# A fused attention and maxout kernel: its hand-ordered queue planned anew, with bias products as units of their own and twelve staging buffers

## The chip, the cores and the metric

The kernel runs on one core of a Trainium2 chip. The metric is device microseconds of one execution. Its engines are TensorE (PE; its weight loads are shown as PEld), VectorE (DVE), ScalarE (ACT), GpSimd (POOL) and SyncE (SP), whose queue here issues nearly all DMAs. Each engine works through its own instructions in the order in which the program emits them, and waits on semaphores where an instruction needs what another engine has not yet done.

## What is computed

The reference, cut to what matters, is windowed attention with a linear distance bias, followed by a feed-forward layer with the maximum of three products:

```
# q, k, v: [4, 8, 768, 64]; n_global = 8, n_local = 96
scores = q @ k.T / sqrt(64)
rel = i - j;  is_local = 0 <= rel < 96;  is_global = j < 8
dist = 96 where (is_global and not is_local), else |rel|
scores = scores - slope[head] * dist          # slope[h] = 2 ** -(h + 1)
a = softmax(scores where (is_global or is_local) else -1e9)
x = (a @ v) as [3072 tokens, 512]
h = max(x @ w1, x @ w2, x @ w3)               # w*: [512, 768]
out = h @ w_out                               # [3072, 512], fp32
```

## The kernel before

The 3072 tokens are 24 tiles of 128 (six for each of the four batches). The feed-forward layer takes them in seven chunks, `SIZES = [4, 2, 2, 4, 4, 4, 4]` tiles. All the work is cut into units, and the string `SCHEDULE` (line 24) lists every unit in the order of emission; the last loop of the kernel function reads a unit's letter, its numbers and, behind `@`, the number of the buffer it takes, and calls the function of that letter. So the string fixes the order on every engine and all the buffers. It was made by a planner outside the kernel, from costs of the units. The units (first numbers: G is a group of two tiles, T a tile, g one half of the heads, c a chunk, f one of six blocks of 128 hidden columns, j which of w1, w2, w3; a last number without a point of its own is the engine: 0 ScalarE, 1 VectorE, 2 GpSimd):

- `l`: load of q (0), k (1) or v (2) of a group; group 12 ("quad") is tiles 0 to 3 of q and k in four loads of 0.5 MB. `c`: its cast to bf16; on GpSimd a cast is two instructions. `v`: cast of v into the tile's buffer.
- `x` (TensorE) and `y` (copy): transposes of q and k; from group 5 on `X`, a DMA transpose on SP, does both.
- `K`, `B`: masks and biases of a head, at the start. `S`: scores of a tile and half of the heads. With its last number 1, two matmuls with the identity first put the bias into the two PSUM banks; without it, `m` multiplies the mask in after the exponential. `e`: exponential (ScalarE).
- `G`, `V`: put the first keys and values of the batch into a tile's buffers, after the tile's own S or A has read them and before the next tile's.
- `A`: probabilities times values. `n`: reciprocal and scaling (VectorE). `t` and `u`, or the DMA transpose `Z` on SP: the transpose that makes x ready for the chunk's F.
- `w`, `q`: loads of the weights (w0.j is 0.5 MB, w1.j is 1 MB, q 0.5 MB); `W`, `Q`: their casts.
- `F`: four matmuls, into one bank. `f` with j = 0 casts the bank to SBUF, with j = 1 takes the maximum with it, with j = 2 the maximum again, into the chunk's hidden buffer.
- `O`: six matmuls, an output tile. `o`: its copy into a staging buffer. `s`: its store, on SP; with a last 2, in two halves. `E`: the output tiles of the last chunk; the last of them is cut into columns of 256, 128 and 128, and the last copy and store are ScalarE's own.
- `D`: matmuls of zeros at the start. `R`: the distances.

PSUM has eight banks. F, O, x and t take one, A and S take two; a bank can be taken again once its last reader is done. Staging buffers of the outputs are slices of the buffers `wst0` and `wst1`, into which the weights were loaded (three each).

## Time and profile before

| | |
|---|---|
| median of 3 runs | 176.38 us (176.31 to 176.66) |
| the profiled execution's own time | 176.6 us |
| its span, first to last instruction | 174.7 us |
| granted TensorE clock | 1.000 |
| DMA | 37.35 MB, mean 214 GB/s |

In a profile, a group of instructions is given by line, engine, operation, tile and shape, with the number of them, the busy time and the mean duration of one in ns, and then the time that the engine idled before them and what ended it. In a timeline the first number is the start in us, the second how long the merged instructions took. A matmul's busy time includes its drain, so that two matmuls in a row overlap in it.

### The profile page before, as it was taken

To read this page: it belongs to the slowest core of one execution; us is meant where nothing else is said; L and a number is where in the kernel's file an instruction comes from. 1 tells how busy PE (TensorE), PEld (TensorE's weight loads), DVE (VectorE), ACT (ScalarE), POOL (GpSimd) and SP (SyncE) were. 2 spreads that over 40 slices of the span, in tenths; PEclk is the share of its full clock that TensorE was granted. 3 is DMA by queue.
4 is the path that set the end of the run, shared out by engine and by line. 5 is a ranking of instruction groups with operands and counts; after the bars stand their busy time and mean duration, and the time that the engine had idled before them with its cause. 6 is when DMAs were issued, how large, how long until landed. Compare 5 with 4: busy or idle time off the path is not lost.

```text
span 174.7 us, 3862 instructions
## 1 busy us (share of the span) xinstructions
PE 166.9 (96%) x1489; PEld 93.5 (54%) x1510; DVE 127.7 (73%) x259; ACT 102.4 (59%) x153; POOL 48.9 (28%) x94
## 2 busy tenths in 40 slices
...
GB/s 148 352 292 312 363 351 379 294 319 345 270 230 267 193 145 194 290 319 198 232 146 196 119 253 200 290 159 260 272 184 68 32 90 64 0 180 240 60 10 234
DMA packets 66658, 37.35 MB, mean 214 GB/s; under 512 B 24144, under 2 KB 61904, under 8 KB 66640
## 3 DMA queue, kind: packets, MB, share of 16 engines
...
q8 instruction: 12, 0.20, 0.5%
q10 hardware_dynamic: 144, 0.07, 0.1%
q14 instruction: 6, 0.05, 0.1%
...
## 4 chain that ended last, share of the span: by engine, by line
PE 83%; DVE 5%; DMA 4%; ACT 3%; issue 2%; SPq 1%; ACTq 0%
PE psum L405 50%; PE psum L429 18%; PE psum L321 5%; DMA rawqq<-in_q_dram 4%; PE psum L363 4%; PE psum L366 3%; PE psum L258 2%; DVE qkT L266 1%; ACT P L328 1%; PE psum L390 1%; DVE h L421 1%; DVE P L337 1%; PE psum L313 1%; SPq L213 1%; ACT qb L185 1%
## 5 line engine op out<-in xcount | busy, mean ns | idle before, releaser
L405 PE MATMUL psum<-xT,w 128*128 128x512 bf16 (+1 forms) x491 | 99.3, 348 | 1.1
L405 PEld LDWEIGHTS <-w 128*128 128x128 bf16 x504 | 47.5, 98 | 43.1 <-issue 2.7
L328 ACT ACTIVATE P<-psum 128x1024 bf16<-128x1024 f32 (+1 forms) x48 | 43.3, 953 | 13.5 <-PE psum L321 13.2
L421 DVE TENSOR_TENSOR h<-h,psum 128x512 bf16<-128x512 bf16 (+1 forms) x42 | 24.6, 604 | 16.1 <-PE psum L405 12.6
L429 PE MATMUL psum<-wo,ht 128*128 128x512 bf16 (+2 forms) x148 | 32.9, 362 | 0.6 <-issue 0.3
L337 DVE TENSOR_TENSOR P<-P,wmask 128x1024 bf16<-128x1024 bf16 x35 | 23.8, 695 | 6.2 <-ACT P L328 6.1
L424 DVE TENSOR_TENSOR ht<-h,psum 128x512 bf16<-128x512 bf16 (+1 forms) x42 | 26.1, 643 | 3.0 <-PE psum L405 2.4
L419 ACT CAST h<-psum 128x512 bf16<-128x512 f32 (+1 forms) x32 | 15.6, 517 | 20.1 <-PE psum L405 17.9
L429 PEld LDWEIGHTS <-ht 128*128 128x128 bf16 x156 | 14.0, 98 | 14.1
L238 POOL CAST va<-rawv 64x512 bf16<-64x512 f32 x26 | 16.5, 636 | 13.6 <-DMA rawv<-in_v_dram 12.8
L375 DVE TENSOR_TENSOR xb<-psum,rz 128x512 bf16<-128x512 f32 x24 | 16.6, 691 | 0.8
L299 POOL COPY va<-vaf 4x260 int32<-4x260 int32 x15 | 5.9, 395 | 37.5 <-PE psum L366 37.2
L321 PE MATMUL psum<-qkT 64*128 64x128 bf16 x352 | 14.9, 217 | 1.2 <-DVE qkT L266 0.9
L321 PEld LDWEIGHTS <-qkT 64*128 64x128 bf16 x352 | 10.3, 94 | 9.6 <-issue 6.8
L363 PEld LDWEIGHTS <-P 128*128 128x128 bf16 x192 | 12.3, 97 | 2.4
L363 PE MATMUL psum<-va,P 128*128 128x65 bf16 x160 | 12.5, 193 | 0.1
L444 ACT COPY ost<-psum 128x512 f32<-128x512 f32 x11 | 6.4, 589 | 8.9 <-PE psum L429 8.2
L366 PEld LDWEIGHTS <-P 128*128 128x128 bf16 x160 | 10.4, 97 | 1.5 <-issue 0.3
L434 ACT COPY ost<-psum 128x512 f32<-128x512 f32 (+2 forms) x5 | 2.3, 480 | 15.1 <-PE psum L429 15.0
L366 PE MATMUL psum<-va,P 128*128 128x65 bf16 x128 | 9.9, 193 | 0.0
L301 ACT COPY va<-vaf 4x520 bf16<-4x520 bf16 x10 | 6.2, 620 | 3.8 <-PE psum L366 3.7
L374 DVE RECIPROCAL rz<-psum 128x8 f32<-128x8 f32 x24 | 4.8, 202 | 4.7 <-PE psum L366 3.7
...
## 6 DMA issues: line engine op xcount, KB each, us to landing
rawv<-in_v_dram SPq DMA_DIRECT2D x12, 512.0 KB, 6.3
rawq<-in_q_dram SPq DMA_DIRECT2D x10, 512.0 KB, 7.3
rawk<-in_k_dram SPq DMA_DIRECT2D x10, 512.0 KB, 7.0
...
wst<-in_moe_w_dram SPq DMA_DIRECT2D x3, 512.0 KB, 8.1
wost<-in_moe_w_out_dram SPq DMA_DIRECT2D x3, 512.0 KB, 7.3
out_dram<-ost SPq DMA_DIRECT2D x9, 128.0 KB, 1.8
```

Of the source, the lines that this page charges most:

```text
L238: copies[how](heads(va(T))[64 * e:64 * e + 64, :, 0:D], src)
L321: nc.tensor.matmul(sp[:, hh, j2, ds], qT(T - ds, 1)[hsl, jp], qT(T, 0)[hsl, jp], start=not how, stop=True, skip_group_check=True)
L328: nc.scalar.activation(P[:, :, 0:n], sps[T, g].rearrange("p a b d n -> p (a b) d n")[:, :, 0:n], AF.Exp, bias=0.0, scale=scale)
L337: mul(P, P, wmask[:, g, :, 0:2])
L363: nc.tensor.matmul(o, P[:, i, 0], heads(va(T))[:, h], start=True, stop=(t == 0), skip_group_check=True)
L366: nc.tensor.matmul(o, P[:, i, 1], heads(va(T - 1))[:, h], start=False, stop=True, skip_group_check=True)
L375: nc.vector.tensor_tensor(out=x.rearrange("p (g h) d -> p g h d", g=2), in0=o4[:, :, :, 0:64], in1=rz[:, :, :, None].to_broadcast([128, 2, ...
L405: nc.tensor.matmul(ps, w123[f // 2][:, j, dm, (f % 2) * 128:(f % 2) * 128 + 128], xT[c][:, dm], start=(dm == 0), stop=(dm == 3))
L419: copies[how](h01, ps)
L421: nc.vector.tensor_max(h01s[c, f], h01s[c, f], ps)
L424: nc.vector.tensor_max(dst, h01s[c, f].rearrange("p (t e i) -> p t e i", e=2, i=64), ps.rearrange("p (t e i) -> p t e i", e=2, i=64))
L429: nc.tensor.matmul(po, ht[c][:, f, tt * 128:(tt + 1) * 128], wo[:, f, cols], start=(f == 0), stop=(f == NF - 1))
```

## The change

1. A new unit `b` holds the two bias matmuls. `S` with a last number 1 takes the buffer of its `b`; seven groups have one, as before, but tile 0 has one (it had two) and tile 1 has two (it had one).
2. Outputs are staged in a ring `os` of 12 buffers, which lie in one tile with `wst0` and `wst1` (over the place of `wst1`). E takes twelve in turn too.
3. Groups 0 and 1 keep q and k in an order with the half of the heads outside the tile, so that `y` writes one piece.
4. The whole string is another. The planner that made it now holds each buffer until the instruction that reads it last has ended.

Both strings hold the same units but for the seven `b`; tile 8 goes by `Z` and no longer by `t`, and tile 7 the other way (before: tiles 0 to 6, 8 and 11 by `t`; after: 0 to 7 and 11). Counts by engine:

| unit | before: ScalarE, VectorE, GpSimd | after |
|---|---|---|
| `c` cast of q, k | 9, 7, 8 | 5, 6, 13 |
| `v` cast of v | 8, 6, 34 | 10, 6, 32 |
| `y` copy of transposes | 8, 6, - | 5, 9, - |
| `G` | 4, 6, 10 | 7, 10, 3 |
| `V` | 10, 7, 15 | 12, 4, 16 |
| `u` | 3, 6, - | 5, 4, - |
| `f` with j = 0 | 32, 10, - | 24, 18, - |
| `o` | 11, 9, - | 10, 10, - |
| `W` | 2, 4, 3 | 1, 4, 4 |
| `Q` | 1, -, 2 | -, -, 3 |
| `B` | 2, 6, - | 3, 5, - |

The diff, cut (of the string: the start with the first loads and the first F, chunk 3's F, and the end):

```diff
-    l0.12.1@0 l1.12.1@1 R K4 K3 K6 B4.1 B0.1 K5 K0 K2 B1.0 K7 B6.0 B2.1 l1.12.0@2 B3.1 c0.12.1.1@0 B7.1
-    l0.12.0@3 l2.0.2@0 l2.1.2@1 l0.2.2@4 c1.12.1.1@1 l1.2.2@5 w0.1@0 B5.1 D10.512@0 w0.0@1 x12.0.1@0
...
-    v2.1.1 v2.0.1 A0@0 n0@0 v3.0.2 l2.2.2@2 w1.1@1 A1@4 V1.1.2 e2.0@5 v3.1.2 n1@1 S3.0.1@6 c0.2.2.0@2 V1.0.1
-    S3.1.1@0 w1.2@2 t1@2 c1.2.2.1 u1.1@0 e3.0@6 A2@4 n2@2 x2.0.2@3 V2.1.2 V2.0.2 x2.1.2@2 G3.2 y2.1.2.1@2
-    e3.1@7 l1.3.2@6 A3@0 t2@4 l0.3.2@0 y2.0.2.0 W0.1.2 n3@3 t0@3 u2.0 S4.0.0@6 u0.1 e4.0@1 S4.1.0@4 t3@2
-    u3.1 W0.0.1 G4.2 S5.0.0@0 W0.2.2 e5.0@3 S5.1.0@6 m5.0.1 V3.1.0 e5.1@0 m5.1.1 m4.0.1 W2.0.1 v5.0.2 e4.1@2
-    W1.0.1 F0.0.1@2 F0.1.1@3 F0.0.0@0 f0.0.0.0@0 F0.1.0@1 F0.0.2@4 F0.1.2@0 f0.1.0.0@1 F0.4.0@1 v5.1.2
...
-    V22.0.2 n22@0 O4.3@1 V22.1.0 A23@2 n23@3 Z22 O5.3@0 o5.3.0@2 O5.2@4 O5.1@0 O5.0@2 o5.0.0@0 Z23 F6.2.0@3
...
-    f6.0.1.1 f6.0.2.1 f6.3.2.1 s4.0.2 s4.3.2 s5.2.2 F6.5.0@0 f6.5.0.1@0 F6.5.1@3 f6.5.1.1 F6.5.2@1 f6.5.2.1 E@0
+    l1.12.1@0 l0.12.1@1 R B6.1 K6 K7 B1.1 B4.0 K4 B3.1 K1 K5 c1.12.1.1@0 B7.1 B5.0 K3 K2 B2.1 l0.12.0@2
+    l1.12.0@3 D10.512@0 x12.1.1@0 l2.0.2@0 v1.1.2 v1.0.2 v0.1.2 c0.12.1.1@1 D3.256@1 x12.0.1@1 b1.1@2
+    l2.1.2@1 y1.1.1.1@0 b2.1@4 v0.0.2 c0.12.0.1 x12.0.0@6 y0.1.1.1@1 y0.0.1.0 S1.1.1 y1.0.1.0 B0.0 S0.1.0@0
...
+    l0.2.2@5 w1.0@0 w0.1@0 G0.1 m0.1.1 G1.1 b0.0@2 S0.0.1 e1.0@2 v3.1.2 v3.0.2 b2.0@6 e0.0@3 v2.1.1 S2.0.1
+    e2.0@4 v2.0.1 l2.2.2@2 K0 S2.1.1 e2.1@5 w0.0@1 b3.1@0 w0.2@2 w1.1@1 A0@2 G2.1 n0@0 S3.1.1 e3.1@6 A1@6
+    n1@1 b3.0@2 S3.0.1 w1.2@2 c1.2.2.2@2 V1.0.1 c0.2.2.2 e3.0@7 x2.1.2@4 V1.1.1 A2@0 t0@5 y2.1.2.1@2 t1@6
+    n2@2 V2.0.0 x2.0.2@4 y2.0.2.1 u0.0@0 G3.0 u1.0 V2.1.2 A3@2 V3.1.2 l1.3.2@6 n3@3 t2@5 S4.0.0@0 S4.1.0@6
+    l0.3.2@0 V3.0.2 G4.2 l1.4.2@1 e4.0@0 u2.1 t3@4 W2.0.2 u3.0 W1.0.1 m4.0.1 e4.1@3 S5.0.0@2 l2.3.2@0
+    l0.4.2@2 S5.1.0@0 W0.1.1 e5.1@1 m4.1.1 v4.0.2 e5.0@2 v4.1.2 F0.3.0@4 F0.5.0@5 f0.5.0.0@0 F0.4.0@6
...
+    m13.0.1 l1.8.2@2 v15.0.2 F3.4.0@3 F3.1.2@5 l0.8.2@4 v12.0.2 v15.1.2 F3.1.0@4 F3.1.1@2 A12@0 f3.1.0.1@4
+    f3.1.1.1 n12@1 m13.1.1 F3.0.0@4 c0.7.2.1@0 l0.9.2@3 F3.2.0@2 f3.4.0.1@2 f3.0.0.1@0 F3.0.1@0 v16.1.1
+    c0.8.2.2@2 c1.7.2.0 A13@6 F3.4.1@1 F3.2.2@3 f3.1.2.1@1 F3.5.0@4 F3.5.1@5 f3.0.1.1 f3.4.1.1 X14@3
+    F3.2.1@0 f3.2.0.0@3 F3.4.2@1 c0.9.2.2@1 f3.5.0.1@1 l1.9.2@5 f3.5.1.1 n13@0 F3.3.0@2 X15 f3.4.2.1
+    f3.2.1.1 f3.2.2.1 S14.0.0@4 e14.0@5 v17.0.2 S14.1.0@6 F3.0.2@0 F3.3.2@1 f3.3.0.1@4 m14.0.1 f3.0.2.1
+    F3.5.2@2 l2.9.2@0 v16.0.1 c1.9.2.0 e14.1@6 Z13@1 c1.8.2.2 F3.3.1@0 G14.0 S15.0.0@4 e15.0@0 S15.1.0@6
...
+    f5.0.2.1 m23.1.1 f5.5.1.1 A23@5 n22@1 f5.5.2.1 n23@2 f5.2.2.1 O4.3@0 F5.3.2@1 s0.2 s1.0 Z22 O4.2@5
+    f5.3.2.1 O5.3@1 O5.0@2 o5.0.1@0 Z23 o4.2.1@11 o5.3.1@10 O5.1@3 o4.3.1@8 s4.0 F6.0.2@2 F6.2.1@1 F6.0.0@0
...
+    s5.1 s0.0 F6.2.2@7 s5.0 f6.2.2.1 F6.4.2@1 s4.2.2 s5.3.2 s4.3.2 f6.4.2.1 F6.1.2@0 F6.5.0@3 f6.0.2.1
+    f6.1.1.1 F6.5.1@1 f6.1.2.1 F6.5.2@2 f6.5.0.0@2 f6.5.1.1 f6.5.2.1 E@7 O5.2@2 o5.2.0@1 s5.2.2
...
-RINGS = {'r': 7, ... 'wst0': 3, 'wst1': 3, 'ht': 2, 'h01': 5, 'rz': 4}
-LAST_BANKS = (7, 6, 4, 5, 2, 0, 3, 1)
-LAST_STAGES = ((2, 1, 0), (2, 0, 1))
+RINGS = {'r': 7, ... 'wst0': 3, 'wst1': 3, 'ht': 2, 'h01': 5, 'rz': 4, 'os': 12}
+LAST_BANKS = (5, 4, 7, 6, 3, 0, 1, 2)
+LAST_STAGES = (6, 9, 2, 5, 3, 7, 4, 0, 11, 10, 8, 1)
...
+    staging = persist.tile([128, 2048 * RINGS["wst1"] + 1024 * RINGS["wst0"]], FP32, name="staging")
+    staged = {"wst1": (0, 2048), "os": (0, 512), "wst0": (2048 * RINGS["wst1"], 1024)}
...
+            shape = [128, 2, 2, 2, NP // 2, 128] if G < 2 and QUAD_USED else [128, 2, 2, NP, 128]
...
-    def u_S(slot, T, g, how):
-        t = T % NT
+    def u_b(slot, T, g):
+        n = 2 if T % NT else 1
         sp = ring("sp", slot, [128, 2, 2, 2, 128], FP32, "sp")
         sps[T, g] = sp
-        n = 2 if t else 1
-        biased[T, g] = how
-        if how:
-            for hh in range(2):
-                nc.tensor.matmul(sp[:, hh, :, 0:n], identb,
-                                 bias[:, g, hh, :, 0:2] if t else bias[:, g, hh, :, 2:3],
-                                 start=True, stop=False, skip_group_check=True)
+        for hh in range(2):
+            nc.tensor.matmul(sp[:, hh, :, 0:n], identb, bias[:, g, hh, :, 0:2] if n == 2 else bias[:, g, hh, :, 2:3],
+                             start=True, stop=False, skip_group_check=True)
+
+    def u_S(slot, T, g, how):
+        n = 2 if T % NT else 1
+        biased[T, g] = how
+        if not how:
+            sps[T, g] = ring("sp", slot, [128, 2, 2, 2, 128], FP32, "sp")
+        sp = sps[T, g]
...
-        osts[c, tt] = ring(("wst0", "wst1")[chunks[c][tt] % 2], slot, [128, DM], FP32, "ost")
+        osts[c, tt] = ring("os", slot, [128, DM], FP32, "ost")
```

More of the change, by code (lines that the diff above doesn't have):

```diff
@@ L157, in ring @@
         assert 0 <= slot < RINGS[name]
+        if name in staged:
+            first, width = staged[name]
+            first += slot * width
+            flat = staging[:, first:first + math.prod(shape[1:])]
+            return flat if len(shape) == 2 else flat.rearrange("p (i f) -> p i f", i=shape[1])
         return pools[name].tile(shape, dtype, name=label, tag=f"{name}{slot}")
```

143 lines of the change are left out of this document (73 added, 70 removed).

## The prediction

> **What bounds the kernel now.** I read the page's first part, then its chain, then the timeline of TensorE.
>
> ```profile
> span 174.7 us, 3862 instructions
> PE 166.9 (96%) x1489; PEld 93.5 (54%) x1510; DVE 127.7 (73%) x259; ACT 102.4 (59%) x153; POOL 48.9 (28%) x94
> ...
> PE 83%; DVE 5%; DMA 4%; ACT 3%; issue 2%; SPq 1%; ACTq 0%
> ...
> L405 PEld LDWEIGHTS <-w 128*128 128x128 bf16 x504 | 47.5, 98 | 43.1 <-issue 2.7
> ...
> rawk<-in_k_dram SPq DMA_DIRECT2D x10, 512.0 KB, 7.0
> ```
>
> TensorE is busy for 96% of the span and is 83% of the chain that ended last. "Busy" hides short waits, because a matmul counts until it is drained, so I compare the work with the clock instead.
>
> ```profile
> 1.19 4.45 PE L506 MATMUL psum<-zeros 128*128 128x512 bf16 x10 [1.19 <-DVE cap L524]
> 5.60 0.77 PE L252 MATMUL psum<-identb,qbq 128*128 128x128 bf16 x8
> ...
> 21.52 7.94 PE L405 MATMUL psum<-xT,w 128*128 128x512 bf16 x35
> 29.31 0.19 PE L363 MATMUL psum<-va,P 128*128 128x65 bf16 x1
> ...
> 29.79 2.75 PE L405 MATMUL psum<-xT,w 128*128 128x512 bf16 x11
> ...
> 37.73 0.61 PE L258 MATMUL psum<-identb,qb 128*128 128x128 bf16 x8
> 38.18 1.47 PE L405 MATMUL psum<-xT,w 128*128 128x256 bf16 x12
> ...
> 72.66 2.53 PE L405 MATMUL psum<-xT,w 128*128 128x512 bf16 x10
> ...
> 118.58 9.16 PEld L405 LDWEIGHTS <-w 128*128 128x128 bf16 x43 [0.20 <-issue]
> ```
>
> ```profile
> 52.86 0.22 PE psum L390 x4
> ...
> 98.71 0.55 PE psum L321 x16
> ...
> 169.63 1.93 PE psum L429 x20
> ```
>
> In an unbroken run 43 weight loads take 9.16 us: (9.16 - 0.098) / 42 = 0.216 us for a matmul of 512 columns. The 504 matmuls of F (144 of them half as wide) and the 24 output tiles of six are 576 such widths: 124.3 us. From the first F, at 21.52 us, to the last matmul, at 171.55, there are besides 15 tiles of S at 0.55 us and three of half that (9.1), 17 A at 29.79 - 29.31 = 0.48 and three halves (8.9), four x at 0.45 (1.8) and five t at 0.22 (1.1). Together 145.2 us of 150.0: only **4.8 us** are lost in the body. The rest of the span is 21.5 us of start and 3.1 us of tail.
>
> **The change, part by part.** *Work.* Both queues hold the same units: 126 F, 24 output tiles, 48 S, 24 A, 10 x, 9 t. So TensorE's 145.2 us stand, and only start, losses and tail can move. Bias products: two of the seven groups covered tile 0 (half width), now one does, so two matmuls grow by 256 columns: 2 x 0.108 = 0.2 us, issued while TensorE waits for casts: nothing.
>
> *Start.* ScalarE and VectorE set it.
>
> ```profile
> 10.00:15.00 5.00, 4.58 (x67) 2.49 (x67) 4.43 (x9) 4.31 (x8) 3.59 (x7) 1.00 1.20 290
> 15.00:20.00 5.00, 4.99 (x97) 3.62 (x94) 4.83 (x12) 4.69 (x6) 3.33 (x8) 1.00 1.11 341
> ```
>
> ```profile
> 15.40 1.05 ACT L185 CAST qb<-rawq 128x1024 bf16<-128x1024 f32 x1
> 16.34 1.95 ACT L328 ACTIVATE P<-psum 128x1024 bf16<-128x1024 f32 x2
> ...
> 20.90 0.42 DVE L393 COPY xT<-psum 128x512 bf16<-128x512 bf16 x1 [0.30 <-PE psum L390]
> ...
> 11.20 1.88 DVE L266 COPY qkT<-psum 128x512 bf16<-128x512 bf16 x3
> ...
> 22.38 1.69 POOL L185 CAST w<-wst 128x512 bf16<-128x512 f32 x2 [1.67 <-DMA wst<-in_moe_w_dram]
> ...
> 32.09 1.05 ACT L185 CAST w<-wst 128x1024 bf16<-128x1024 f32 x1 [1.45 <-DMA wst<-in_moe_w_dram]
> ```
>
> (Windows: busy us of TensorE, weight loads, VectorE, ScalarE, GpSimd.) VectorE is busy for 9.3 and ScalarE for 9.0 of these 10 us. The first F waits for the last u of chunk 0, which hangs on e of tile 3 (ends 18.29). The new queue gives the cast of q of group 2 (1.05 us, ScalarE) to GpSimd and puts one more bias row (about 0.4) and one G less (0.2) on ScalarE: e3 ends near 17.45. Then ScalarE has V2, u0, G3, u1 and e4.0 (0.6 + 0.55 + 0.2 + 0.55 + 0.95, estimates from row means less 0.05 of overlap) before u3 (0.59): F could start at about 20.9. But the 1 MB load w1.0 now stands ahead of the three w0 loads and feeds the first F. The old queue's landings, from the two casts that wait for them: 5.5 MB (counted from the first load) at 22.38 us, 9 MB at 32.09, so 2.8 us for a MB; w1.0 is complete at 5 MB, 21.0 us, and its cast takes 0.7: 21.7. Between 20.6 and 21.7 I take 21.1: **-0.4 us** (ends -0.9, +0.2). The later weights stay at 9 MB, so this lead cannot grow by them.
>
> *F of chunks 0 to 2 (to 72.66 us).* Work there by the same prices is 49.2 us of 51.1: 1.9 lost. I followed the new queue by hand, bank by bank, with the row means: TensorE waits about 1.4 us by whole durations, less where instructions overlap (three copies of 0.682 take 1.88 us: 0.60 apart). With 0.1 at each of six entries to S I take 1.4: **-0.5** (ends -1.3, +0.5). Holding a buffer until its reader has ended is a rule for the planner: it removes no instruction, and pays only where an S or F now waits for a bank.
>
> *F of chunk 3.* Five of six first casts of a bank (f with j = 0) go to VectorE, before it was one; ScalarE idles there.
>
> ```profile
> L337 DVE TENSOR_TENSOR P<-P,wmask 128x1024 bf16<-128x1024 bf16 x35 | 23.8, 695 | 6.2 <-ACT P L328 6.1
> L424 DVE TENSOR_TENSOR ht<-h,psum 128x512 bf16<-128x512 bf16 x30 | 21.0, 724 | 2.6 <-PE psum L405 2.1
> L421 DVE TENSOR_TENSOR h<-h,psum 128x512 bf16<-128x512 bf16 x30 | 19.9, 681 | 15.0 <-PE psum L405 12.6 <-ACT h L419 2.0
> ...
> L419 DVE CAST h<-psum 128x512 bf16<-128x512 f32 x9 | 6.2, 684 | 1.4 <-PE psum L405 1.3
> ```
>
> From the first F3 to the one before the last, VectorE has 5 casts (3.4), 5 maxima (3.4), 4 results (2.9), 2 n (1.8), 3 m (2.1), a cast (0.7), a v (0.5) and 1.3 left over from chunk 2: 16.1 us. TensorE has 17 F, two A and an S: 15.9. By whole durations VectorE is the bound, and the walk gives 1.9 us of waiting, most of it where F3.0.2 wants the bank that the maximum f3.2.1 reads; at 0.07 less for each of 24 it has 14.4 us and hides. Nearest row: three copies at 0.60, so the second: **+0.2** (ends 0, +1.9). In the same stretch ScalarE's cast c1.9 waits for a load that SP issues behind the transpose X14; queued behind the cast is e14.1, and S15.1 waits for its banks. By the load's median landing that is covered, by 2 us more it is not: it stays inside the upper end.
>
> *Chunks 4 and 5.*
>
> ```profile
> xT<-xb SPq DMA_TRANSPOSE x15, 3.6
> ```
>
> Covers are as thin as before: after A19 both queues have six F (5.2 us) for n19 and the transpose of its result (3.6 us to landing); X20 now has five stores ahead of it on SP's queue. **0** (ends -0.6, +1.2).
>
> *Last chunk and tail.*
>
> ```profile
> 150.29 16.05 PE L405 MATMUL psum<-xT,w 128*128 128x512 bf16 x71
> ...
> 155.62 3.33 PEld L405 LDWEIGHTS <-w 128*128 128x128 bf16 x16 [0.27 <-issue]
> ...
> 163.59 2.25 PEld L405 LDWEIGHTS <-w 128*128 128x128 bf16 x11 [0.25 <-issue]
> ...
> 171.63 0.27 ACT L434 COPY ost<-psum 128x128 f32<-128x128 f32 x1 [0.34 <-PE psum L429]
> 171.93 0.37 ACTq L435 DMA_DIRECT2D out_dram<-ost  x1
> ...
> 141.39 0.57 SPq L450 DMA_DIRECT2D out_dram<-ost  x1
> ```
>
> ```profile
> L444 ACT COPY ost<-psum 128x512 f32<-128x512 f32 x11 | 6.4, 589 | 8.9 <-PE psum L429 8.2 <-ACT P L328 0.7
> ...
> out_dram<-ost SPq DMA_DIRECT2D x9, 128.0 KB, 1.8
> ```
>
> From 150.29 to 171.55 us stand 18 F and four output tiles, 96 widths: 20.7 of 21.3 us, so 0.5 is lost, at gaps like the two quoted. In the new queue, walked in the same way, one wait of 0.15 is left: **-0.4**. But output tile O5.2 now comes behind E, whose last tile was cut into pieces of 256, 128 and 128 columns to end early. Before: last matmul, 0.08, copy 0.27, issue, 1.8 to landing: 2.2 us. After: 0.08, a whole copy of 0.59, a store of two halves, the second issued 0.55 later, and 1.8: 3.1. **+0.9** (ends +0.6, +1.2). The twelve staging buffers relieve stores that nothing waited for: 0.
>
> Sum: -0.4 - 0.5 + 0.2 + 0 - 0.4 + 0.9 = -0.2 us. The profiled execution took 176.6 us (span 174.7 and 1.9 around it), 0.2 above the median of 176.38; on the median the forecast is **176.2**.
>
> **A rule to weigh.** GpSimd gets 14 more casts (c, W, Q).
>
> ```profile
> L185 POOL CAST w<-wst 128x512 bf16<-128x512 f32 x6 | 4.5, 769 | 2.7 <-DMA wst<-in_moe_w_dram 2.7
> ...
> L185 POOL CAST wo<-wost 128x512 bf16<-128x512 f32 x4 | 2.3, 610 | 2.3 <-DMA wost<-in_moe_w_out_dram 2.3
> ```
>
> One shape takes 0.61 or 0.77 us: something holds it up by 0.16. The Trainium skill (SBUF — State Buffer, Who interferes with whom) says that GpSimd shares a port pair with VectorE as an exclusive lock, so that one of two overlapping instructions stands still; these rows fit that. If many of the casts were held for a whole VectorE instruction, the sum by that rule would be that of the third rival.
>
> **The rivals.** *VectorE takes over in chunk 3* (slower): the 1.9 us instead of 0.2: 176.2 + 1.7 = 177.9. It decides once its 24 instructions stand 15.9 / 24 = 0.66 us apart. For: five casts moved; against: 0.60 in the row above. 0.18.
> *Losses nearly vanish* (faster): 4.8 us down to 15 entries to S at 0.11 (1.7), start -0.9, tail +0.9: -3.1, with half a microsecond that stays: 173.8. For: buffers held to the reader's end are what the waits in the trace are about; against: DMA covers stay thin. 0.23.
> *GpSimd late:* 16 instructions from the landing of w1.2 to the cast of the last w_out at 0.16 each come 2.6 us late; the first output tile, by my walk, has about 1.5 of cover: 176.2 + 1.1 = 177.3. 0.08.
> *The early load of w1.0 buys nothing* (the change does not do what it says): F starts at 21.7 and the reordering wins nothing by chunk 2's end: 176.2 + 0.6 = 176.8. 0.09.
>
> **How the numbers follow.** Forecast 0.42, spread about 175.3 to 177.1. About 0.2%, 0.35 us, is what a measurement can tell. Faster: 0.17 of the forecast and 0.23: 0.40. Same: 0.14 and 0.03: 0.17. Slower: 0.11, 0.18, 0.08, 0.06: 0.43. The range takes half of the fast rival and most of the slow one: 173.6 to 178.3; the likeliest case alone 175.3 to 177.1.
>
> **What would show it.** First L405 matmul at 20.6 to 21.7 us; first F3 before 72.3; VectorE under 4.9 of 5 us through F3; the last matmul 3.9 to 4.2 us before the end of the span (now 3.1); no PE wait for POOL. A single wait of over 1 us on a transpose (X20, Z19, Z15) or on a load that ScalarE awaits (c1.9 before e14.1) would make it wrong.

## The result, and the profile after

The changed kernel is slower: its median is 177.1 us (20 runs, 176.52 to 179.39) beside 176.56 us for the kernel before (20 runs, 176.21 to 177.12), a ratio of 1.0043 with a 95% interval of 1.0026 to 1.0060. The profiled execution took 177.0 us with a span of 175.1, at a granted clock of 1.000. The ratios count fast executions only, which leaves out those over 1.5% above the fastest of their kernel (the one at 179.39 us here, and the profiled one of e2_g_scalar below, whose clock, 0.990 on the mean, fell in one slice behind 53 us and of which, but for the issue of one store, only rows ahead of that are used).

The page of the changed kernel, first its engines, then the shares of the chain that ended last:

```profile
span 175.1 us, 3856 instructions
PE 165.8 (95%) x1489; PEld 93.4 (53%) x1510; DVE 136.0 (78%) x268; ACT 93.7 (54%) x145; POOL 56.4 (32%) x100
...
PE 74%; DVE 15%; issue 3%; DMA 3%; ACT 2%; ACTq 1%; SPq 0%; DVEq 0%
```

VectorE has three times its share of the chain (15%, before 5%). Its busy time is up by 8.3 us, GpSimd's by 7.5, ScalarE's down by 8.7. That is more than moved work: at the mean durations of the kernel before, the units that VectorE gained, less those that it gave away, are some 6 us (an estimate from its rows). The rest is single instructions that grew (below). The timeline of TensorE gives the terms of the prediction's sum; here the first F, the first F of the last chunk, and the last matmuls of the changed kernel:

```profile
22.74 2.55 PE L433 MATMUL psum<-xT,w 128*128 128x512 bf16 x10
...
148.78 1.46 PE L433 MATMUL psum<-xT,w 128*128 128x512 bf16 x6
...
169.81 1.24 PE L457 MATMUL psum<-wo,ht 128*128 128x512 bf16 x5
```

The first F comes at 22.74 (before 21.52): +1.2 us. From there to the first F6 it is 126.04 us; with the 1.30 us of the output tile that now comes behind E, 127.34, where it was 128.77. From the first F6 to the end of the last matmul (169.81 + 1.24 = 171.05) it is 22.27, less 1.30 is 20.97, where it was 21.26. So the body lost 1.7 us less. Behind the last matmul the span goes on for 175.1 - 171.05 = 4.05 us, before 3.15: +0.9. The sum is +0.4, as the spans say (175.1 and 174.7). By the prediction's prices for each unit, the 1.4 us that the body won ahead of F6 divide into 0.3 up to the first F3, 0.2 up to the first F4 and 0.9 in chunks 4 and 5.

| term | predicted | measured |
|---|---|---|
| start | -0.4 | **+1.2** |
| F of chunks 0 to 2 | -0.5 | -0.3 |
| F of chunk 3 | +0.2 | -0.2 |
| chunks 4 and 5 | 0 | -0.9 |
| last chunk | -0.4 | -0.3 |
| tail | +0.9 | +0.9 |
| sum | -0.2 | +0.4 |

**The start.** These are the stretches that the prediction showed of before, and one of chunk 3's F (busy us of TensorE, weight loads, VectorE, ScalarE, GpSimd):

```profile
10.00:15.00 5.00, 4.40 (x58) 2.19 (x56) 4.82 (x9) 4.46 (x7) 3.44 (x6) 1.00 1.20 290
15.00:20.00 5.00, 3.94 (x80) 3.14 (x79) 4.59 (x11) 4.03 (x6) 3.27 (x6) 1.00 1.08 369
78.00:93.50 15.50, 15.39 (x124) 7.70 (x126) 14.51 (x26) 6.46 (x8) 5.87 (x11) 1.00 1.11 238
```

VectorE is nearly full from 10 to 20 us (9.4 of 10) while ScalarE, whose work the prediction summed, has 1.5 us to spare. Through chunk 3's F VectorE is busy 14.5 of 15.5 us and TensorE hardly waits: the rival of chunk 3 did not come. From 10 us up to the first F, every wait of TensorE that the profile lists names VectorE; three of them:

```profile
15.67 0.29 PE L349 MATMUL psum<-qkT 64*128 64x128 bf16 x4 [0.63 <-DVE qkT L315]
...
18.43 0.19 PE L394 MATMUL psum<-va,P 128*128 128x65 bf16 x1 [0.43 <-DVE va L325]
...
21.58 0.40 PE L418 MATMUL psum<-identb,xb 128*128 128x128 bf16 x4 [0.22 <-DVE xb L403]
```

S3.1 waits for G2 (L315), A2 for V1 (L325), t3 for n3. And VectorE's own timeline there:

```profile
12.03 0.60 DVE L313 COPY kg<-qkT 128x32 bf16<-128x32 bf16 x1
...
12.87 0.58 DVE L315 COPY qkT<-kg 128x32 bf16<-128x32 bf16 x1
13.49 1.62 DVE L254 CAST va<-rawv 64x512 bf16<-64x512 f32 x2
15.04 0.57 DVE L315 COPY qkT<-kg 128x32 bf16<-128x32 bf16 x1
...
17.50 0.87 DVE L325 COPY va<-vaf 4x520 bf16<-4x520 bf16 x2
```

The three G take 0.57 to 0.60 us, where this copy took 0.217 on the mean before; the two casts of v take 1.62 together, 1.18 before. GpSimd casts nearly without a pause from 11.33 to 17.9 us at the same time.

**The tail.** ScalarE, SyncE and the end of the changed kernel:

```profile
169.79 0.27 ACT L462 COPY staging<-psum 128x128 f32<-128x128 f32 x1 [0.30 <-PE psum L457]
170.09 1.31 ACTq L463 DMA_DIRECT2D out_dram<-staging  x1
171.52 0.59 ACT L471 COPY staging<-psum 128x512 f32<-128x512 f32 x1 [1.46 <-PE psum L457]
172.13 0.81 SPq L477 DMA_DIRECT2D out_dram<-staging  x2
```

The copy of O5.2 starts 0.47 us behind the last matmul. ScalarE's issue of E's last store, 1.31 us here and 0.37 before, stands ahead of it.

### The profile page after: what moved, and what is told of

Same layout as the page of the kernel before. It is cut to its first block, busy times and chain, and to the rows that moved or that the text cites. A ratio compares the mean times of both kernels' runs of the same rounds, so it can differ in the third digit from the quotient of the medians.

```text
span 175.1 us, 3856 instructions
## 1 busy us (share of the span) xinstructions
PE 165.8 (95%) x1489; PEld 93.4 (53%) x1510; DVE 136.0 (78%) x268; ACT 93.7 (54%) x145; POOL 56.4 (32%) x100
## 4 chain that ended last, share of the span: by engine, by line
PE 74%; DVE 15%; issue 3%; DMA 3%; ACT 2%; ACTq 1%; SPq 0%; DVEq 0%
PE psum L433 46%; PE psum L457 16%; PE psum L349 5%; DMA rawqq<-in_q_dram 3%; PE psum L391 3%; DVE ht L452 3%; DVE h L449 2%; PE psum L394 2%; DVE xb L403 2%; DVE P L365 2%; ACT P L356 1%; PE psum L270 1%; DVE qkT L287 1%; DVE qkT L315 1%; ACTq L463 1%
## 5 line engine op out<-in xcount | busy, mean ns | idle before, releaser
L433 PE MATMUL psum<-xT,w 128*128 128x512 bf16 (+1 forms) x490 | 97.2, 348 | 0.9
L447 ACT CAST h<-psum 128x512 bf16<-128x512 f32 (+1 forms) x24 | 12.0, 516 | 39.5 <-PE psum L433 36.6
L452 DVE TENSOR_TENSOR ht<-h,psum 128x512 bf16<-128x512 bf16 (+1 forms) x42 | 26.7, 645 | 2.1 <-PE psum L433 1.2
L365 DVE TENSOR_TENSOR P<-P,wmask 128x1024 bf16<-128x1024 bf16 x34 | 25.5, 773 | 2.8 <-ACT P L356 2.8
L254 POOL CAST va<-rawv 64x512 bf16<-64x512 f32 x26 | 18.1, 697 | 24.7 <-DMA rawv<-in_v_dram 15.5
L323 POOL COPY va<-vaf 4x260 int32<-4x260 int32 x16 | 6.7, 419 | 30.8 <-PE psum L394 29.4
L447 DVE CAST h<-psum 128x512 bf16<-128x512 f32 (+1 forms) x18 | 11.1, 624 | 2.0 <-PE psum L433 1.9
L201 POOL CAST qb<-rawq 128x512 bf16<-128x512 f32 x14 | 8.5, 633 | 10.9 <-issue 9.7
L325 ACT COPY va<-vaf 4x520 bf16<-4x520 bf16 x12 | 7.5, 623 | 4.4 <-PE psum L394 4.2
```

Of the source, the lines that this page charges most:

```text
L254: copies[how](heads(va(T))[64 * e:64 * e + 64, :, 0:D], src)
L365: mul(P, P, wmask[:, g, :, 0:2])
L433: nc.tensor.matmul(ps, w123[f // 2][:, j, dm, (f % 2) * 128:(f % 2) * 128 + 128], xT[c][:, dm], start=(dm == 0), stop=(dm == 3))
L447: copies[how](h01, ps)
L452: nc.vector.tensor_max(dst, h01s[c, f].rearrange("p (t e i) -> p t e i", e=2, i=64), ps.rearrange("p (t e i) -> p t e i", e=2, i=64))
```

## The experiments

All ratios are to the kernel before on the same chip. The strings are shown by the units that differ.

### The tail undone: e1_tail

```diff
-O5.1@3 o4.3.1@8 s4.0 ... s5.0 ... E@7 O5.2@2 o5.2.0@1 s5.2.2
+O5.1@3 O5.2@7 o4.3.1@8 s4.0 o5.2.0@6 ... s5.0 s5.2.2 ... E@7
```

> The changed kernel with output tile O5.2, its copy and its store moved from behind E to where chunk 5's other output tiles are (bank 7, staging slot 6). Theory 1 (the tail costs 1.1 us, because a whole copy, a store in two halves and the copy's wait behind ScalarE's own store issue come after the last matmul): the last matmul stays near 170.9 us, the end comes 2.2 + 1.0 us after it as before the change, so about 176.0 us, 1.0 to 1.2 below the changed kernel. Rival (the end is set by SP's queue of late stores, not by O5.2): under 0.4 us gained.

Measured: 176.3 us (175.67 to 177.95), ratio 1.0005 (0.9977 to 1.0033). That is some 0.7 us less than the changed kernel by the ratios, under the 1.0 to 1.2 expected, and the two intervals just overlap. The profiled span is 173.9 and the last matmul ends at 168.75 + 1.92 = 170.67: a tail of 3.2 us. The rows of this run's end:

```profile
168.75 1.92 PE L457 MATMUL psum<-wo,ht 128*128 128x512 bf16 x20
...
170.71 0.27 ACT L462 COPY staging<-psum 128x128 f32<-128x128 f32 x1 [0.30 <-PE psum L457]
171.00 0.37 ACTq L463 DMA_DIRECT2D out_dram<-staging  x1
```

By the profile the term of the tail is shown: with the tile back, the tail is 3.2 us again, where before has 3.15 and the changed kernel 4.05.

### The tail alone: e11_before_tail

```diff
-O5.3@1 o5.3.0@2 O5.2@4 O5.1@0 ... o5.2.1@0 ... s5.2.2 ... E@0
+O5.3@1 o5.3.0@2 O5.1@0 ... E@0 O5.2@3 o5.2.0@3 s5.2.2
-'wst0': 3
+'wst0': 4
```

(The first line is cut to the units concerned.)

> The kernel before with one piece of the change alone: the output tile 2 of chunk 5, its copy on ScalarE and its store in two halves behind the last chunk's output tiles (a fourth buffer wst0 holds it). Prediction's step: +0.9 us. Theory now (the copy stands behind ScalarE's own store, too): +0.9 to +1.3 us, last matmul 3.9 to 4.4 us before the end of the span, ScalarE's copy of that tile over 0.4 us behind its last matmul. Rival (the store of the cut last tile ends last in any case): 0 to +0.3.

Measured: 177.91 us (177.48 to 178.76), ratio 1.0095 (1.0075 to 1.0115). The tail is 175.9 - 172.22 = 3.7 us, half a microsecond more than before: under both theories and over the rival. The copy did not wait behind the store, whose issue took 0.37 here. The whole is up by 1.7 us; a good half of the other 1.2 is a wait that the edit itself made:

```profile
147.13 2.75 PE L430 MATMUL psum<-wo,ht 128*128 128x512 bf16 x12 [0.67 <-ACT ost L445]
```

O5.1 takes the bank of O5.3, and with O5.2 gone from between them it waits 0.67 us for ScalarE's copy of O5.3. So this run shows 0.5 us for the tail, and is no measure of the whole time.

### E's last store on SyncE: e5_sp_store

```diff
-                                  (384, 512, nc.scalar.copy, nc.scalar)):
+                                  (384, 512, nc.scalar.copy, nc.sync)):
```

> The changed kernel with E's last small store issued by SP instead of ScalarE. Theory 1: ScalarE's issue of that store (1.31 us, 0.37 before the change) stands ahead of the copy of O5.2; without it the copy starts near 171.0 instead of 171.52 and about 0.5 us comes off. Rival (the copy waits for TensorE): the copy's start stays at 171.5 and the time the same within 0.2.

Measured: 176.52 us (176.03 to 178.11), ratio 1.0024 (1.0002 to 1.0046); the interval overlaps that of the changed kernel. In its profile ScalarE is idle for 1.03 us ahead of the copy of O5.2, and not for 1.46:

```profile
172.01 0.59 ACT L471 COPY staging<-psum 128x512 f32<-128x512 f32 x1 [1.03 <-PE psum L457]
```

With ScalarE's issue at 0.37 (e7_q_scalar, below) the copy waits for the same 1.03. So the issue costs 0.4 us at the end only when it takes over 1.2: in two of the four profiles that have this tail and this store (the changed kernel 1.31, e3_order 1.22; e2_g_scalar and e7_q_scalar 0.37). Tails of 3.7 us go with the short issue, 4.0 with the long one. What lengthens it was not tried. The gain of 0.5 us that was expected for the whole is not clear of noise here.

### Twelve staging buffers alone: e6_staging12

```diff
-RINGS = {... 'ht': 2, 'h01': 5, 'rz': 4}
+RINGS = {... 'ht': 2, 'h01': 5, 'rz': 4, 'os': 12}
-o0.3.1@0 e8.0@2 o0.2.0@0 ... O0.1@1 o0.1.1@1 ... o1.1.0@2
+o0.3.1@0 e8.0@2 o0.2.0@1 ... O0.1@1 o0.1.1@2 ... o1.1.0@3
```

(and so on in turn, with the tile `staging` of the change)

> The kernel before with the new staging alone: twelve buffers taken in turn, the queue as it was. My theory: nothing waited for a staging buffer, so 0: within 0.2% of the kernel before. Rival (a part of the 1.7 us that the body won is due to staging): faster by 0.3 us or more.

Measured: 176.84 us (176.31 to 177.09), ratio 1.002 (1.0006 to 1.0034). There is no gain, so the rival falls; if anything the kernel is slower, by some 0.35 us. TensorE's waits are those of before but for one near 48 us (at F1.3.1), which is 0.5 us in this profile and names VectorE's `h` (L431); what made that late was not followed.

### The three G on ScalarE: e2_g_scalar

```diff
-G0.1 m0.1.1 G1.1 ... S2.1.1 e2.1@5 ... A0@2 G2.1 n0@0
+G0.0 m0.1.1 G1.0 ... S2.1.1 G2.0 e2.1@5 ... A0@2 n0@0
```

> The changed kernel with G0, G1 and G2 on ScalarE instead of VectorE (G2 right behind S2.1). Theory 2 (VectorE's queue is the path of the start, and small copies stand on it for 0.6 us each while GpSimd casts): the copies take 0.22 on ScalarE, S3.1 starts near 15.0 instead of 15.67, first F at 22.0 to 22.4 instead of 22.74, and 0.3 to 0.7 us come off the time. Rival (the first F waits for the 1 MB load of w1.0 and its cast): first F stays at 22.7, no change.

Measured: first F at 22.30 instead of 22.74, time 176.95 us (176.11 to 179.88), ratio 1.005 (1.0018 to 1.0082). The first F lies in the range expected; the gain of time does not come, as the interval overlaps that of the changed kernel. Part of the 0.44 us is luck: this execution's first load came earlier, its first transpose of q and k is at 5.47 and not at 5.62. Counted from that transpose, the first F comes 16.8 us later here and 17.1 in the changed kernel (17.08 to 17.14 in four profiles with this start), so, with 17.0 in e8_three below, which has the same G, ScalarE for G is worth 0.1 to 0.3 us at the start. The timeline of VectorE shows a loss behind the start, in the profiled execution, which was the longest of its twelve:

```profile
44.14 3.00 DVE L367 TENSOR_TENSOR P<-P,wmask 128x512 bf16<-128x512 bf16 x1 [0.59 <-ACT P L356]
47.06 1.09 DVE L365 TENSOR_TENSOR P<-P,wmask 128x1024 bf16<-128x1024 bf16 x1
```

A product of 128x512 (m6.1) took 3.00 us, and TensorE waited 1.8 us for VectorE shortly behind it. In the profile of the changed kernel the same instruction took 0.42, in those of e1_tail 0.86, e3_order 1.69 and e5_sp_store 1.96. GpSimd, in e2_g_scalar, casts through that time:

```profile
44.02 0.61 POOL L254 CAST va<-rawv 64x512 bf16<-64x512 f32 x1
44.58 2.28 POOL L201 CAST wo<-staging 128x512 bf16<-128x512 f32 x4
46.93 0.69 POOL L254 CAST va<-rawv 64x512 bf16<-64x512 f32 x1
```

Four casts of `wo` end one behind another while the product stands, at 0.57 us each: it was held over several of them.

### VectorE's two casts of v later: e3_order

```diff
-e0.0@3 v2.1.1 S2.0.1 e2.0@4 v2.0.1 l2.2.2@2 ... G2.1 n0@0 S3.1.1
+e0.0@3 S2.0.1 e2.0@4 l2.2.2@2 ... G2.1 n0@0 v2.1.1 v2.0.1 S3.1.1
```

> The changed kernel with the two casts of v of tile 2 moved on VectorE from ahead of G2 to behind n of tile 0; no engine changes. Theory 2 in its form that only the order matters (1.6 us of casts stand ahead of G2, for which S3.1 waits): S3.1 at 14.6 to 14.8 instead of 15.67, A1 0.9 earlier, first F 0.3 to 0.9 earlier. In its form that the hold by GpSimd matters: the same casts come later, are held as long, and A2 gets none of it: first F within 0.2. Rival (w1.0): no change.

Measured: 177.38 us (176.66 to 178.73), ratio 1.0061 (1.0039 to 1.0082). S3.1 no longer waits, but the next one does, for the same engine:

```profile
18.59 0.19 PE L394 MATMUL psum<-va,P 128*128 128x65 bf16 x1 [1.22 <-DVE va L325]
...
22.90 2.33 PE L433 MATMUL psum<-xT,w 128*128 128x512 bf16 x9
```

A2 waits 1.22 us for V1 instead of 0.43, and the first F is at 22.90, 17.3 us behind the first transpose instead of 17.1. This order on VectorE wins nothing: the wait moves on to the work that was put later.

The run settles one more thing. The change also gave these tiles another layout, and that could be why the copies of G take 0.57 to 0.60 us. Here the same copy, of tile 2 in the same new layout, takes 0.18 us, at the end of one of GpSimd's casts and with none of VectorE's own casts ahead of it:

```profile
13.98 0.18 DVE L315 COPY qkT<-kg 128x32 bf16<-128x32 bf16 x1 [0.57 <-PE psum L349]
```

So it is not the layout that makes them long.

### Neighbours by themselves: e4_port

Six of VectorE's forms, alone and beside a train of GpSimd casts, written as small loops:

```diff
+        for kind in kinds:
+            for _ in range(N):
+                kind()
...
+        for kind in kinds:
+            for _ in range(N):
+                nc.gpsimd.tensor_copy(g16, p32[:, 0:512])
+                kind()
```

> Leaves out the whole computation and writes zeros. VectorE's kinds of instruction stand eight times each alone, then eight times each beside a train of GpSimd casts (128x512 fp32 to bf16): a copy of 128x32 (as G), a cast of 64x512 (as v), a cast of 128x1024 (as W), a product of two tiles in SBUF (128x1024, as m), a maximum of one tile in SBUF with one in PSUM (as f), a copy from PSUM (as y). Theory (GpSimd's casts hold VectorE's instructions off one by one): the kinds that read and write SBUF alone take 1.3 to 3 times as long beside the train, the small copy the most by ratio (0.2 us alone, 0.4 to 0.7 beside), and single instructions are held for a whole cast or more (over 0.5 us above their time alone); the two kinds that read PSUM change by under 10%. GpSimd's own casts go from about 0.6 to 0.7 us or above. Rival (it is the order and the semaphores in the kernel that make them long, not the neighbour): all six kinds as long beside the train as alone, within 10%.

The groups of the stretch without GpSimd (5.9 to 34 us):

```profile
...
L44 DVE TENSOR_TENSOR m<-a,b 128x1024 bf16<-128x1024 bf16 x8 | 5.5, 691 | 0.2
...
L47 DVE TENSOR_TENSOR h<-a,ps 128x512 bf16<-128x512 bf16 x8 | 5.5, 686 | 0.2
L38 DVE CAST v<-f 64x512 bf16<-64x512 f32 x8 | 3.3, 418 | 0.2
L35 DVE COPY kgd<-kgs 128x32 bf16<-128x32 bf16 x8 | 1.4, 173 | 0.2
```

and with it (39.9 to 80 us):

```profile
L72 POOL CAST g<-p 128x512 bf16<-128x512 f32 x48 | 35.1, 731 | 3.1 <-DVE y L69 0.4
L44 DVE TENSOR_TENSOR m<-a,b 128x1024 bf16<-128x1024 bf16 x8 | 8.1, 1008 | 0.2
...
L38 DVE CAST v<-f 64x512 bf16<-64x512 f32 x8 | 5.5, 690 | 0.2
...
L47 DVE TENSOR_TENSOR h<-a,ps 128x512 bf16<-128x512 bf16 x8 | 5.5, 687 | 0.2
L35 DVE COPY kgd<-kgs 128x32 bf16<-128x32 bf16 x8 | 2.7, 336 | 0.2
```

The four forms that stay within SBUF grow: the small copy from 173 to 336 ns, the cast of v from 418 to 690, W's from 692 to 958, the product from 691 to 1008. The two that read PSUM do not move (686 and 687, 690 and 690). GpSimd's cast goes from 613 (the eight alone) to 731. The rival falls. These are means: single copies beside the train take from 0.17 to 0.59 us, so the 0.57 to 0.60 of G in the kernel is what a copy takes when it is held, and not more. The Trainium skill (SBUF — State Buffer, Who interferes with whom) has just this division: the pair of ports is shared between VectorE and GpSimd, held for a whole instruction, and not needed by a VectorE instruction with one input in SBUF outside the two-port modes; these rows agree.

### Spaced products: e12_spaced, and a train without gaps: e13_overlap

```diff
+                nc.scalar.copy(flat[:, 0:w], src[:, 0:w])
+                kind()
...
+        for _ in range(64):
+            nc.gpsimd.tensor_copy(g16, p32[:, 0:512])
```

> Leaves out the whole computation and writes zeros. Ten mask products of 128x1024 and ten of 128x512 with strides (as for the first tile of a batch), each behind a ScalarE copy of another width, first alone, then beside an unbroken train of GpSimd casts. Theory A (where VectorE has no instruction waiting while a cast runs, GpSimd's next casts go first and the product is held for several of them): single products of 1.5 to 3 us beside the train, 0.4 to 0.7 alone. Theory B (the two engines alternate in any case): no product over its time alone plus one cast, that is 1.3 us; then the 3.00 us of the run with G on ScalarE needs something more than a train of casts.

Measured: the ten products of 128x1024 take 0.69 us alone and 0.69 to 1.13 beside the train; those of 128x512 take 0.42 or 0.43 alone and 0.43 to 0.87 beside it. Theory B holds. In e13_overlap each cast has a tile of its own:

```diff
-        for _ in range(64):
+        for g16 in gs:
```

> Leaves out the whole computation and writes zeros. As the run with spaced mask products, but each of the 64 GpSimd casts writes a tile of its own, so that one follows the other without a gap (in that run all wrote one tile, 0.068 us apart). Theory A2 (it is the gap between two casts that lets VectorE in; without one a product is held until the train ends): products of 1.5 us and more, up to the length of the train that is left. Theory B (the engines alternate even so): none over 1.3 us, as with gaps.

Measured: at most 1.16 us. The row of this run's longest product:

```profile
32.36 1.16 DVE L28 TENSOR_TENSOR P<-P,wm 128x1024 bf16<-128x1024 bf16 x1 [1.17 <-ACT P L36]
```

Both forms of theory A fall. A product takes at most 0.47 us more than alone (1.16 less 0.69), with gaps or without. So in these runs a product is held for less than the 0.61 us of one cast, and the 3.00 us need something else that they do not have.

### w_out's casts on ScalarE: e7_q_scalar

```diff
-c0.3.2.0 Q0.2 ... v8.0.2 F1.2.1@3 Q1.2 ... f0.2.2.1 S6.1.0@0 Q2.2 e6.1@4
+y3.0.2.0 Q0.0 ... e7.0@6 Q1.0 ... y4.0.2.0 Q2.0
```

> The changed kernel with the three casts of w_out (Q) taken from GpSimd and given to ScalarE, after y of group 3, e7.0 and y of group 4. Theory (the train of GpSimd casts from 38 to 48 us holds off VectorE's mask product m6.1 by a random time): m6.1 takes 0.4 to 0.9 us, F1.1.0 waits under 0.3 us, the spread of the runs shrinks from some 3 to about 1 us, and the median falls by 0.3 to 0.6 us against the changed kernel (ratio to the kernel before 0.999 to 1.002). Rival (the spread comes from the landings of DMAs): spread and median stay, ratio 1.003 to 1.006.

Measured: 176.46 us (176.2 to 177.0), ratio 1.0002 (0.9989 to 1.0016). That is 0.7 us under the changed kernel by the ratios, a little more than expected, and the intervals do not overlap. The spread shrinks from 2.5 us (176.52 to 179.03) to 0.8. m6.1 takes 0.58:

```profile
44.07 0.58 DVE L367 TENSOR_TENSOR P<-P,wmask 128x512 bf16<-128x512 bf16 x1 [0.33 <-ACT P L356]
...
169.87 0.37 ACTq L463 DMA_DIRECT2D out_dram<-staging  x1
170.87 0.59 ACT L471 COPY staging<-psum 128x512 f32<-128x512 f32 x1 [1.03 <-PE psum L457]
```

So the spread of the changed kernel came with the casts of w_out as it has them, on GpSimd, and the rival (loads) falls. The other runs agree: with these casts on GpSimd the spreads are 2.1 to 2.3 us (e1_tail, e3_order, e5_sp_store), with them on ScalarE 0.8 to 1.3 (this run and e8_three, e15_start, e16_start_a1, e17_a1_first below). The edit also gives the casts other places in the queue, and no run takes engine and place apart. Why a product beside them was held for 3.00 us is not shown. The profiled execution of the changed kernel has hardly any of this cost (m6.1 took 0.42 there), so the sum of +0.4 in the table above does not hold it, while the ratio of the medians stands for 0.8 us.

### Three edits together: e8_three

The edits of e1_tail, e2_g_scalar and e7_q_scalar in one string.

```diff
-G0.1 G1.1 G2.1 Q0.2 Q1.2 Q2.2 ... E@7 O5.2@2 o5.2.0@1 s5.2.2
+G0.0 G1.0 G2.0 Q0.0 Q1.0 Q2.0 ... O5.2@7 o5.2.0@6 s5.2.2 ... E@7
```

> The changed kernel with three edits together: the output tile 2 of chunk 5 back ahead of the last chunk, with its copy and store, G of groups 0 to 2 on ScalarE, and w_out's casts on ScalarE. Theory (the three prices are separate and add): tail -0.8 us, start -0.4, train of casts -0.4: 1.6 us less than the changed kernel, 175.4 to 175.8, ratio to the kernel before 0.992 to 0.997. Rival (what one edit wins is waited for again at the next thin place, a DMA landing or VectorE in chunk 3): 176.2 or above, no better than the tail edit alone.

Measured: 175.54 us (175.13 to 176.43), ratio 0.9949 (0.9933 to 0.9965), 0.94% or 1.7 us under the changed kernel, where 1.6 was forecast. The gains measured one by one, 0.7 (e1_tail), none that is clear (e2_g_scalar) and 0.7 (e7_q_scalar), come to 1.4, so within the noise they add. Its first F is at 22.41, 17.0 us behind the first transpose.

### Group 2's casts on GpSimd, alone: e10_before_gp

```diff
-c0.2.2.0@2 ... c1.2.2.1
+c0.2.2.2@2 ... c1.2.2.2
```

> The kernel before with one piece of the change alone: the casts of q and k of group 2 go from ScalarE and VectorE to GpSimd. My prediction's step (ScalarE, relieved of a 1.05 us cast, is early, and the first F with it): first F at 21.0 to 21.3, time -0.2 to -0.4 us. Theory now (GpSimd's casts hold VectorE's small instructions, and GpSimd itself takes 1.2 us for each): VectorE's copies of V and its product and casts between 15 and 19 us grow by 0.1 to 0.4 us each, first F at 21.5 to 22.3, time 0 to +0.7 us.

Measured: 177.91 us (177.66 to 178.0), ratio 1.0086 (1.0073 to 1.0099). First F at 22.62, 1.1 us later; both are worse than either of the two forecasts. TensorE names GpSimd twice on the way:

```profile
18.81 0.40 PE L259 MATMUL psum<-identb,qb 128*128 128x128 bf16 x4 [0.16 <-POOL qb L186]
19.72 0.19 PE L367 MATMUL psum<-va,P 128*128 128x65 bf16 x1 [0.48 <-POOL va L300]
22.62 2.55 PE L406 MATMUL psum<-xT,w 128*128 128x512 bf16 x11
```

In the queue of before the casts push V2, on the same engine, behind them, and A3 waits. The prediction's step (relief of ScalarE, earlier F) has the wrong sign there; and it is GpSimd's lateness that costs, rather than the held VectorE (its V1 takes 0.66 us instead of 0.27, but A2 is hardly late).

### The old start with the new queue: e9_old_to53 and e14_old_to53b

The units of the kernel before up to its e9.0, with `b` directly ahead of its S, then all that is left of e8_three's string; buffers that live across the seam get the new number. In the second run the seam is mended:

```diff
-m9.1.1 S9.0.0@4 G9.1 e9.0@1 F1.3.2@6 f1.3.2.1 F1.1.2@7 f1.1.2.1 ... A8@0 V8.1.0 O1.1@5 ... F2.2.0@4 F2.3.0@2
+S9.0.0@4 e9.0@1 F1.3.2@6 F1.1.2@7 f1.3.2.1 f1.1.2.1 m9.1.1 G9.1 F2.2.0@2 F2.3.0@3 ... A8@0 V8.1.0 O1.1@5
```

> The queue of the kernel before up to its e9.0 (about 55 us, with the old order of the start and of chunks 0 and 1), from there the changed queue, with the output tile 2 of chunk 5 back ahead of the last chunk. Theory (the change's start costs 1.2 us by itself, its gains lie behind 55 us and in the tail as it was): first F at 21.5, about 1.2 us lost to 60 us as before, then the changed kernel's waits: 174.6 to 175.2, ratio to the kernel before 0.990 to 0.994. Rival (the late start is no loss of its own, since a later landing or VectorE would hold up an earlier F as well): 175.5 or above, no better than the kernel with the three edits.

Measured: 175.93 us (175.31 to 176.32), ratio 0.9972 (0.996 to 0.9984). First F at 21.30, but at the seam TensorE waits for chunk 1's last maxima (1.25 us at O1.1). So this run settles nothing, by a fault of the seam. With the seam mended:

> The same joint of the two queues (kernel before up to 55 us, changed queue behind it) with the seam mended: the last maxima of chunk 1 stand ahead of tile 9's mask product and two F of chunk 2 ahead of A8, so that O1.1 finds its input. The first joint lost 0.52 and 1.42 us there. Theory (the old start is worth what it gains): first F at 21.3 to 21.5, at most 1.6 us lost by 64 us, 174.2 to 174.9, ratio 0.987 to 0.992. Rival (an earlier body meets later landings, the lead is lost by 60 to 110 us): 175.4 or above.

Measured: 174.77 us (174.54 to 175.59), ratio 0.9891 (0.9869 to 0.9913). First F at 21.43. Against e8_three, whose body behind the seam and whose tail it shares, that is, by the ratios, 0.6% or 1.0 us less, which is what the first F says (22.41 - 21.43). It suggests that the loss of the start is kept to the end and that the old start would have won it back, but it does not show it. The units ahead of the seam are in the old order all through, not at the start alone. And the profiled execution, the longest of its six at 175.59, ends no earlier than that of e8_three: its span is 173.8 beside 173.5, and two waits for transposes by DMA take the lead back between 55 and 103 us:

```profile
PE psum L433 <- DMA xT<-xb: 0.7, 1, 0.7
PE psum L349 <- DMA qkT<-qb: 0.5, 1, 0.5
```

By its median this is the fastest kernel of the study, 1.1% under the kernel before.

### Inside the new start: e15_start, e16_start_a1, e17_a1_first

e15_start gives e8_three the old engines for group 2's casts and V1. e17_a1_first only puts A1 and n1 ahead of S3.1 in e8_three. e16_start_a1 does both.

```diff
-c1.2.2.2@2 V1.0.1 c0.2.2.2 e3.0@7 x2.1.2@4 V1.1.1 A2@0 t0@5 y2.1.2.1@2 t1@6 n2@2 V2.0.0 x2.0.2@4 y2.0.2.1
+c0.2.2.0@2 V1.1.2 V1.0.1 c1.2.2.1 e3.0@7 A2@0 t0@5 t1@6 x2.0.2@7 x2.1.2@4 n2@2 V2.0.0 y2.0.2.1@2 y2.1.2.1
...
-A0@2 n0@0 S3.1.1 e3.1@6 A1@6 n1@1
+A0@2 n0@0 A1@6 n1@1 S3.1.1 e3.1@6
```

> The kernel with the three edits, and besides the casts of q and k of group 2 on ScalarE and VectorE, as in the kernel before, with V1 in halves on GpSimd and VectorE (as before) and the transposes behind them in the order q, k. Theory (giving these two casts to GpSimd is what the start lost by, as it cost the kernel before 1.1 us at the first F): A2 waits under 0.3 us (0.9 in the kernel with the three edits), first F at 21.4 to 22.0, 0.4 to 1.0 us less than that kernel: 174.6 to 175.2. Rival (with the other order the bound is VectorE's or ScalarE's sum of work, or the landing of w1.0): first F at 22.3 or later, 175.5 or above.

Measured: 175.54 us (175.38 to 176.26), ratio 0.993 (0.9909 to 0.9952). First F at 22.91. This execution's first load came 0.5 us later, its first transpose is at 5.97 instead of 5.43; counted from there the first F comes 16.95 us later beside 17.0 in e8_three, so it is no better. The theory falls and the rival stands: A2 now waits 0.20 us for ScalarE's exponential instead of VectorE, and e3.0 stands behind the cast of q, which keeps ScalarE from 17.38 us for 1.07.

> The kernel of the run before with group 2's casts on ScalarE and VectorE, and besides A1 and n1 ahead of S3.1 in the queue. Theory (TensorE works in order: A1, which has all it needs, stands behind S3.1, which waits 0.86 us for G2; n1, V1 and A2 follow late): A1 about 0.7 us earlier, A2 and the first F 0.4 to 0.8 us earlier (22.1 to 22.5 where that run had 22.91), time 0.3 to 0.7 us less. Rival (S3.1 and its exponential are the path, not A1): first F within 0.2 us of that run's or later, since S3.1 now stands behind A1.

Measured: 175.6 us (175.31 to 176.19), ratio 0.9934 (0.9912 to 0.9957). First F at 22.65, behind the 22.1 to 22.5 expected, so the rival stands here too; W1.0's cast on VectorE is among the waits, with 0.2 us.

> The kernel with the three edits (group 2's casts stay on GpSimd), and besides A1 and n1 ahead of S3.1. Theory: as in the run beside it, but V1's two copies on VectorE still run beside GpSimd's casts (1.05 us for the two), so A2 gains about 0.5 and the first F 0.2 to 0.6 us on the 22.41 of that kernel; time 175.0 to 175.4. Rival: first F within 0.2 us of 22.41 or later.

Measured: 175.48 us (174.91 to 176.12), ratio 0.9929 (0.9904 to 0.9953). First F at 22.00, 16.3 us behind the first transpose of q and k, where it is 17.0 in e8_three, 16.9 in e16_start_a1, 15.9 in the kernel before and 17.1 in the changed one. So, with the casts on GpSimd, 0.7 of the start's 1.2 us were A1 standing behind S3.1, which waited for G2, when A1's own input was there. With the casts on the old engines the same order wins next to nothing (16.95 in e15_start, 16.9 in e16_start_a1). And with A1 ahead, the casts are better off on GpSimd (16.3 against 16.9): there the prediction's step had the right sign. In time, the intervals of e8_three and e17_a1_first overlap; the profile shows one wait that came instead, the longest of TensorE between 99 and 103 us of this run:

```profile
PE psum L433 <- DMA xT<-xb: 0.8, 1, 0.8
```

F4.5.1 waits for Z15. The SyncE rows of this run and, below them, of e8_three:

```profile
96.80 3.98 SPq L424 DMA_TRANSPOSE xT<-xb  x2
```

```profile
96.84 2.69 SPq L424 DMA_TRANSPOSE xT<-xb  x2
```

Issued at the same time, the two transposes keep SyncE 1.3 us longer. It is one of the thin covers that the prediction listed, and it differs from profile to profile: 2.67 us in the changed kernel, 3.08 in e16_start_a1, 4.07 in e15_start, 4.48 in e14_old_to53b with its wait of 0.7 us.

## Why the prediction went wrong

**The step that failed is the start**, -0.4 us. It took ScalarE's list of work as the path ("e3 ends near 17.45"). Its e3.0 ends at 18.47:

```profile
17.45 1.02 ACT L356 ACTIVATE P<-psum 128x1024 bf16<-128x1024 f32 x1 [0.35 <-PE psum L349]
```

ScalarE waits there for TensorE, which waited for VectorE. The stretches that the prediction quoted had VectorE at 9.3 of 10 us, more than ScalarE, and the change gave it G of tiles 0 to 2 and both halves of V1; no VectorE walk was made for the start. Being full is not enough to show it, as VectorE is 9.4 of 10 us busy after the change; what shows it are the waits, which name G2 and V1. Of the 1.2 us, TensorE's order at A1 and S3.1 is worth 0.7 as long as the casts are on GpSimd (e17_a1_first), G on VectorE 0.1 to 0.3 by itself (e2_g_scalar); the two meet in the same wait, so they need not add, and what is left is not divided further.

**The casts of w_out on GpSimd** are the other loss. The sum had no term for them; they stood only in the rival of GpSimd being late. With them on ScalarE the kernel takes 0.7 us less by the ratios (e7_q_scalar), and on GpSimd they ran beside the products of VectorE that were held longest.

**The time of 177.1** lies inside the stated range, at the upper end of the likeliest case, and that is luck: the start was out by 1.6 us and the body by 1.0 the other way. Of the signs named, the first F (22.74 against 20.6 to 21.7) and the first F3 (some 73.5 against under 72.3) failed, and VectorE in chunk 3, the last matmul's distance from the end and the absence of waits for GpSimd held.

**The load of w1.0** was on time: it landed at 20.4 us, and W1.0 is cast at 21.77 right behind VectorE's u2, with no wait for a DMA. That rival is out. Its own price was also summed too low: a start of +0.2 instead of -0.4 and nothing won by reordering, -0.5, come to 1.1 us and so to 177.3, where 176.8 was written.

**The body** was right in sign and too small: -1.7 instead of -0.7, most of it in chunks 4 and 5, where the prediction took 0 and reached to -0.6. The staging alone won nothing (e6_staging12), which leaves the order, the rule on held buffers and the moved casts. The profile of before lists no wait of 0.15 us or more for a bank's reader behind the first F, which speaks against the rule; no run takes these apart, and the cause stays open.

**Chunk 3:** VectorE was near its bound (14.5 of 15.5 us) and still kept up with TensorE. The rival at 177.9 has no wait to show at its place.

**The tail** was right in sign. Its size, +0.9, came out exactly with the help of a long issue of ScalarE's store (1.31 us) that the prediction did not have; with the short issue of 0.37 the tail is 3.7 us long, +0.5 to +0.6, at or under the prediction's lower end.

**The rule on the shared port** was weighed the wrong way round: GpSimd was to be late. No wait of TensorE names GpSimd in the changed kernel; VectorE was the one held. The means of its groups went up: the product of 128x1024 from 695 ns to 773, W's cast from 686 to 855, v's cast from 470 to 546 and G's copy from 217 to 357.

```profile
L365 DVE TENSOR_TENSOR P<-P,wmask 128x1024 bf16<-128x1024 bf16 x34 | 25.5, 773 | 2.8 <-ACT P L356 2.8
...
L195 DVE CAST w<-staging 128x1024 bf16<-128x1024 f32 x4 | 3.4, 855 | 0.0
L254 DVE CAST va<-rawv 64x512 bf16<-64x512 f32 x6 | 3.3, 546 | 0.1
L315 DVE COPY qkT<-kg 128x32 bf16<-128x32 bf16 x8 | 2.9, 357 | 0.0
```
